# All scores of a pair in one four-bank tile, with wide exponentials and another order of the attention loop

## The chip, the cores and the metric

The kernel runs on one core of a Trainium2 chip. The core has a matrix engine (TensorE, called PE in the profile, with its weight loads as PEld), a vector engine (VectorE, DVE), a scalar engine (ScalarE, ACT), GpSimd (POOL) and a sync engine (SP) that issues DMAs. Each engine works through its own list of instructions in order; semaphores make one engine wait for another. Matmul results land in PSUM[...]. Everything else lives in SBUF. The metric is the device time in microseconds (us).

## The reference

Two parts follow each other. The first is attention in chunks: for each of 4 batches and 8 heads (768 positions, 64 dimensions), each chunk of 32 queries sees 8 memory rows, 16 positions before it, its own 32 and 8 after it.

```python
q_c   = q[:, :, c_start:c_end]
k_full = concat([mem_k, k[:, :, max(0, c_start-16):min(S, c_end+8)]])   # v_full likewise
a   = softmax(q_c @ k_full.T / sqrt(64))
out[:, :, c_start:c_end] = a @ v_full
```

The second is a gated MLP on the 128 tokens of each batch that score highest. With x the attention output as (4, 768, 512), per batch:

```python
scores  = x @ w_gate                     # (768,)
top_idx = argpartition(-scores, 128)[:128]
xe = x[top_idx]
ye = relu(xe @ w1) @ w2                  # 512 -> 1024 -> 512
out[top_idx] = xe + sigmoid(scores[top_idx])[:, None] * ye
```

## The kernel before

**Pairs.** The attention works on pairs of heads: 16 pairs n, four to a batch. Three groups of 16 transposes on TensorE bring q, k and v of a pair into the layout that the matmuls want. `tr_q(n)` writes p_q and ScalarE copies it to qT (L219). `tr_k(n)` writes p_t and VectorE copies it to kw (L232), into which GpSimd puts the memory keys (`mem_cols`, L224). `tr_v(n)` writes p_t and ScalarE copies it to vw (L242). `back_v(n)` transposes vw once more into p_v, and VectorE copies it to vc (L251). p_q and p_v share one buffer (pool pvv, tag "pv"); p_t is a single tile.

**Scores and values.** `scores(n, half)` multiplies keys and queries of four of the eight groups, 8 matmuls into a two-bank tile p_s, of which there are two, and then runs three exponentials on ScalarE (L271), one for each of the three positions c of a chunk in a group, since each c has its own mask as bias. Each covers 256 elements per partition and writes es. `values(n, half, fills)` multiplies es with vc into the one-bank tile p_w (12 matmuls, L292; its ones column gives the sums), and VectorE takes the reciprocal rd (L295) and writes the normalized rows to x (L296). `fills` asks for a matmul of zeros ahead of it (L116).

**The order of the loop.** The order on every engine is the order in which the program emits its work. Per pair n it is: scores(n+1, 0), tr_q(n+2), values(n, 0), tr_k(n+2), scores(n+1, 1), back_v(n+1), values(n, 1), tr_v(n+2). Loads of q, k and v in units of two pairs are issued by GpSimd four units ahead, with a cast from fp32 to fp16; the weights w1 and w2 come on the same queue.

**The MoE part between.** `hook(i)` stands at eight places of each pair, i = 8n to 8n+7, and emits the steps of `moe_steps(b)` that are due there. For a batch b they begin at the first pair of the next batch: six dot products with w_gate (junk, L335, VectorE), rows of the scores by transposes into brow (L346, copied by ScalarE, L352), the gate (an exponential on ScalarE, then four small VectorE steps, L361 to L365), six comparisons (gr, L373), 37 counting matmuls (L380, L383), mask and incl (L389, L391), slot and sel (L398, L405), then the indices (aux, L438; idx, L441) and an indirect DMA that gathers the 128 rows (xe, L412). Later come `m_rows` (transposes of xe, L419, copied to xeT by ScalarE), `m_ffn1` in two halves (L453; hT by ScalarE, L455) and `m_ffn2` (L462; y by ScalarE, L465), and a DMA that adds y to the output (L466). All these use a single one-bank tile p_m (`m_bank`, pool pmm); for the last batch, LAST, they use p_s tiles. `m_x16` (L340, ScalarE) makes an fp16 copy of x of the last batch, half of it at pair 14.

**The tail.** After pair 15 GpSimd issues the store of the last batch's x. VectorE does the dot products of LAST in two halves: the first two pairs' columns inside pair 15 (scrA), the rest after the loop (scrB), then their sum (L581). `m_rows` and the FFN of batch 2 stand there in TensorE's list ahead of counts, gather by matmul and FFN of LAST.

Of the kernel before, what the change touches and what calls it, by code (L numbers as in the profile page):

```python
# [26 lines left out]
def kernel(  # L27
# [13 lines left out]
    nc = tc.nc  # L41
# [9 lines left out]
    NB = 6  # L51
    HD = S * D
    NPR = B * NP
    SLOTS = 4
# [3 lines left out]
    att = ctx.enter_context(tc.tile_pool(name="att", bufs=4))  # L58
    xpool = ctx.enter_context(tc.tile_pool(name="xp", bufs=2))
    mod = ctx.enter_context(tc.tile_pool(name="mod", bufs=2))  # L60

    pss = ctx.enter_context(tc.tile_pool(name="pss", bufs=2, space=bass.MemoryType.PSUM))
    pxx = ctx.enter_context(tc.tile_pool(name="pxx", bufs=1, space=bass.MemoryType.PSUM))
    pvv = ctx.enter_context(tc.tile_pool(name="pvv", bufs=1, space=bass.MemoryType.PSUM))
    ptt = ctx.enter_context(tc.tile_pool(name="ptt", bufs=1, space=bass.MemoryType.PSUM))
# [83 lines left out]
    vcs, kws, vws = [], [], []  # L149
# [63 lines left out]
    def tr_q(n):  # L213
        if n >= NPR:
            return
        p_q = pvv.tile([128, 8, 128], F16, tag="pv", name="p_q")[:, :, 0:96]
        transposes(q16s, n, p_q)
        qT = att.tile([128, 96, 8], F16, tag="qT", name="qT")
        nc.scalar.copy(out=qT, in_=p_q.rearrange("p j t -> p t j"))  # L219
        qTs[n] = qT  # L220
# [32 lines left out]
    GROUPS = ((0, 1, 2, 6), (3, 4, 5, 7))  # L253
    ess = {}

    def scores(n, half, fills=0):
        if n >= NPR:
            return
        kw, qT = kws[n % SLOTS], qTs[n]
        qf = qT.rearrange("p t j -> p (t j)")  # L260
        p_s = pss.tile([128, 2, 512], FP, tag="ps", name="p_s")
        fill_into(p_s[:, 0, :], fills)
        for gi, g in enumerate(GROUPS[half]):
            for h in range(2):
                o = 64 * h
                nc.tensor.matmul(out=p_s[:, h, 96 * gi:96 * gi + 96], lhsT=kw[o:o + 64, g, :],  # L266
                                 rhs=qf[o:o + 64, 96 * g:96 * g + 96], start=True, stop=True)
        es = att.tile([128, 2, 4, 96], F16, tag="es", name="es")
        pv = p_s[:, :, 0:384].rearrange("p s (g t) -> p s g t", t=96)
        for c in range(3):  # L270
            nc.scalar.activation(out=es[:, :, :, 32 * c:32 * c + 32], in_=pv[:, :, :, 32 * c:32 * c + 32],  # L271
                                 func=AF.Exp, bias=maskb[:, c:c + 1], scale=0.125)
        ess[n, half] = es

    xs = {}

    def values(n, half, fills=0):
        b, pr = divmod(n, NP)
        if pr == 0 and half == 0:
            xs[b] = xpool.tile([128, NB, Dm], FP, tag="x", name=f"x{b}")  # L280
        es, vc = ess.pop((n, half)), vcs[n % SLOTS]
        if n == NPR - 1:
            p_w = pss.tile([128, 2, 512], FP, tag="ps", name="p_w")[:, 0, :]
        else:
            p_w = pxx.tile([128, 512], FP, tag="px", name="p_w")
        fill_into(p_w, fills)
        p_x = p_w[:, 0:390].rearrange("p (i h c) -> p i h c", i=3, h=2)
        for r0, r1, gis in ((0, 96, (0, 1, 2)), (96, 128, (3, 3, 3))):
            for i, gi in enumerate(gis):
                q0, q1 = (0, 96) if gi < 3 else (32 * i, 32 * i + 32)  # L290
                for h in range(2):
                    nc.tensor.matmul(out=p_x[r0:r1, i, h, :], lhsT=es[:, h, gi, q0:q1],  # L292
                                     rhs=vc[:, GROUPS[half][gi], h, 0:65], start=True, stop=True)
# [10 lines left out]
    mods = [MS() for _ in range(B)]  # L304
    outf = out.rearrange("b s d -> (b s) d")
    LAST = B - 1

    def m_bank(b, shape, dt=FP):

        if b == LAST:  # L310
            t = pss.tile([128, 2, 512], FP, tag="ps", name="p_l")
            return t
        return pmm.tile([128, 1, 512], FP, tag="pm", name="p_m")

    def m_store(b):
# [13 lines left out]
    def m_dot(b, bls, pr0=0, pr1=NP, dst=None):  # L329
        m, x = mods[b], xs[b]  # L330
        dst = m.scr if dst is None else dst
        for bl in bls:
            c0, c1 = 2 * D * pr0, 2 * D * pr1
            junk = mod.tile([128, Dm], FP, tag="junk", name="junk")
            nc.vector.scalar_tensor_tensor(out=junk[:, c0:c1], in0=x[:, bl, c0:c1], scalar=1.0, in1=wgb[:, c0:c1],  # L335
                                           op0=ALU.mult, op1=ALU.mult, accum_out=dst[:, bl:bl + 1])

    def m_x16(b, lo, hi, pr0=0, pr1=NP):
        c0, c1 = 2 * D * pr0, 2 * D * pr1
        nc.scalar.copy(out=mods[b].x16[:, lo:hi, c0:c1], in_=xs[b][:, lo:hi, c0:c1])  # L340
# [128 lines left out]
    def moe_steps(b):  # L469

        st = {}

        def at(i, f, *a):
            st.setdefault(i, []).append(lambda: f(b, *a))

        at(0, m_alloc)
        p = dict(dots=(0, 3, 6, 7, 8, 11), row0=13, row1=16, gate=17, cmps=(18, 19, 22, 23, 24, 27),
                 counts=(30, 30, 30, 31, 31, 31), mask=31, slot=34, sel=35, fetch=37, rows=54, ffn=(55, 57, 59))
        if b == LAST - 2:
            p.update(rows=46, ffn=(47, 48, 50))  # L480
        if b == LAST - 1:
            p = dict(dots=(0, 1, 3, 4, 6, 7), row0=9, row1=11, gate=12, cmps=(13, 14, 15, 17, 18, 19),
                     counts=(21, 21, 21, 22, 22, 22), mask=22, slot=24, sel=24, fetch=24)
        for i in range(NB):
            at(p["dots"][i], m_dot, (i,))
        at(p["row0"], m_row, 0, 4)
        at(p["row1"], m_row, 4, 6)
        at(p["row1"], m_gate_exp)
        at(p["gate"], m_gate)
        for i in range(NB):  # L490
            at(p["cmps"][i], m_cmp, (i,))
        for i in range(NB):
# [18 lines left out]
    def hook(i):  # L511
        for f in places.get(i, ()):
            f()
# [7 lines left out]
    fill(2)  # L521
    tr_v(0)
    fill(3)
    scores(0, 0)
    mem_rows(memv16, memvT)
    for n in range(3):
        mem_cols(vws[n], memvT, n)
    tr_q(1)
    fill(2)
    tr_k(1)  # L530
    scores(0, 1)
    fill(2)
    back_v(0)
    tr_v(1)
    fill(2)
    late_constants()
    scrA = mod.tile([128, NB], FP, tag="scrA", name="scrA")
    scrB = mod.tile([128, NB], FP, tag="scrB", name="scrB")
    for n in range(NPR):
        b, pr = divmod(n, NP)  # L540
        i = 8 * n
        nf = 0 if b == 0 or n in (10, 11, 13, 14) else 1
        if b >= 1 and pr == 0:
            m_store(b - 1)
        if n == 1:
            nc.sync.dma_start(out=wgb, in_=_dap(moe_w_gate, 0, [[0, 128], [1, Dm]]))
        if n == NPR - 2:
            m_alloc(LAST)
        scores(n + 1, 0)
        hook(i)  # L550
        if n == NPR - 1:
            m_dot(LAST, range(NB), 0, 2, scrA)
        if 3 <= n + 3 < NPR:
            mem_cols(vws[(n + 3) % SLOTS], memvT, n + 3)
        tr_q(n + 2)
        hook(i + 1)
        values(n, 0, nf)
        hook(i + 2)
        tr_k(n + 2)
        hook(i + 3)  # L560
        scores(n + 1, 1)
        if n == NPR - 2:
# [75 lines left out]
```

## Time and profile before

| | |
|---|---|
| device time, median of 3 runs | 139.72 us (138.43 to 141.23) |
| span of the profiled run | 137.4 us |
| busy, PE / DVE / ACT / POOL | 111.7 / 87.5 / 80.0 / 50.5 us |
| exponentials (L271) | 96, 38.8 us, 485 ns each |
| copies vw, qT on ScalarE | 962 and 813 ns each |
| one of pairs 1 to 3 | 4.67 us |
| pairs 4 to 7 | 22.1 us |
| last x of pair 15 | 111.9 us |

The busy times say how much each engine has to do; the waits say which engine stands still for which. An engine's idle time matters only if what it does next is awaited by others, so the table has to be read with the order of work above: a pair's time is the longest ring of waits through the engines, and that ring differs from the plain pairs of batch 0 to the pairs that carry MoE steps.

### The profile page before, as it was taken

What the parts mean: (1) busy time and instruction counts of PE and PEld (TensorE: products, weight loads), DVE (VectorE), ACT (ScalarE), POOL (GpSimd) and SP (SyncE); (2) the same over time, 40 slices, a digit from 0 to 9 for tenths busy, and PEclk for the clock granted to TensorE, in tenths of its full rate; (3) what the DMA queues carried; (4) which work ended last, traced back from release to release, by engine and by line L of the source; (5) the groups of instructions that cost most, each with busy time, mean ns of one, the idle gap of its engine ahead of it and who ended that gap; (6) DMA issues with size and microseconds to landing.
All of it is one profiled execution on the core that took longest, in us unless ns stands there. A gap on an engine that the chain in (4) does not pass through costs nothing.

```text
span 137.4 us, 4727 instructions
## 1 busy us (share of the span) xinstructions
PE 111.7 (81%) x2024; PEld 83.0 (60%) x2024; DVE 87.5 (64%) x280; ACT 80.0 (58%) x159; POOL 50.5 (37%) x84
## 2 busy tenths in 40 slices
PE   6997688977998978989997999897797897888500
PEld 2355376866777756867885858685656555458100
DVE  3444556574799399889738955997954896651000
ACT  4047958779779859565676947858748005153300
POOL 6996364352683634914200226121004140040130
PEclk9999999999999999995599999999999559999995
DMA  2999999999999999999991002973001439606050
GB/s 63 173 146 184 203 206 206 205 212 206 205 248 287 278 208 206 205 235 290 286 185 23 0 7 19 268 252 43 0 5 12 67 38 260 203 0 81 0 70 6
DMA packets 15397, 19.90 MB, mean 145 GB/s; under 512 B 848, under 2 KB 11536, under 8 KB 15376
## 3 DMA queue, kind: packets, MB, share of 16 engines
q0 software_dynamic: 12832, 14.62, 63.4%
q1 hardware_dynamic: 2544, 4.98, 11.0%
q8 instruction: 16, 0.26, 0.7%
q14 instruction: 5, 0.04, 0.1%
HBM read 24.25 MB, written 7.34 MB: 230 GB/s over the span
## 4 chain that ended last, share of the span: by engine, by line
PE 31%; DVE 15%; ACT 14%; issue 14%; DMA 14%; POOL 6%; POOLq 1%
ACT es L271 7%; DMA q<-in_q_dram 7%; PE p_w L292 7%; PE p_t L210 5%; PE p_v L250 4%; DMA xe<-out_dram,idx 3%; DMA out_dram<-y,idx 3%; DVE junk L335 3%; DVE x L296 3%; ACT qT L219 3%; PE p_w L116 3%; PE p_m L462 3%; PE p_m L453 2%; DVE gr L373 2%; PE p_m L383 2%
## 5 line engine op out<-in xcount | busy, mean ns | idle before, releaser
L271 ACT ACTIVATE es<-p_s,maskb 128x256 f16<-128x256 f32 x96 | 38.8, 485 | 3.2 <-PE p_s L266 3.1
L292 PEld LDWEIGHTS <-es 128*32 128x32 f16 (+1 forms) x384 | 22.1, 116 | 4.4 <-issue 0.7
L292 PE MATMUL p_w<-vc,es 128*32 128x65 f16 (+1 forms) x384 | 24.4, 208 | 0.0
L242 ACT COPY vw<-p_t 128x960 f16<-128x960 f16 x16 | 15.4, 962 | 14.5 <-PE p_t L210 14.5
L224 POOL COPY kw<-memkT 128x64 f16<-128x64 f16 x12 | 8.0, 666 | 36.4 <-DVE kw L232 36.4
L296 DVE TENSOR_TENSOR x<-p_w,rd 128x384 f32<-128x384 f32 x32 | 17.8, 558 | 1.1
L219 ACT COPY qT<-p_q 128x768 f16<-128x768 f16 x16 | 13.0, 813 | 7.4 <-PE p_q L210 7.4
L335 DVE SCALAR_TENSOR_TENSOR junk<-x,wgb 128x512 f32<-128x512 f32 (+1 forms) x30 | 16.2, 582 | 0.0
L466 POOL DMA_INDIRECT out_dram<-y,idx x4 | 6.5, 1635 | 24.7 <-ACT y L465 23.4
L295 DVE RECIPROCAL rd<-p_w 128x6 f32<-128x6 f32 x32 | 6.1, 191 | 12.5 <-PE p_w L292 12.1
L373 DVE TENSOR_SCALAR gr<-brow,scr 128x768 f16<-128x768 f32 x24 | 14.0, 623 | 0.1
L116 PE MATMUL p_f<-zeros 128*128 128x512 f16 x36 | 12.8, 496 | 1.3 <-DVE zeros L110 1.3
L250 PE MATMUL p_v<-ident,vw 128*128 128x128 f16 x128 | 10.2, 225 | 4.3 <-ACT qT L219 4.3
L251 DVE COPY vc<-p_v 128x1024 f16<-128x1024 f16 x16 | 11.0, 687 | 4.3 <-PE p_v L250 4.1
L232 DVE COPY kw<-p_t 128x1024 f16<-128x1024 f16 x16 | 10.9, 683 | 3.5 <-PE p_t L210 3.4
L266 PE MATMUL p_s<-qT,kw 64*128 64x96 f16 x256 | 11.3, 209 | 0.3 <-POOL kw L224 0.3
L250 PEld LDWEIGHTS <-vw 128*128 128x128 f16 x128 | 8.1, 100 | 5.6 <-issue 4.1
L116 PEld LDWEIGHTS <-zeros 128*128 128x128 f16 x60 | 5.9, 110 | 8.9 <-issue 4.6
L210 PE MATMUL p_q<-ident,q 96*64 96x96 f16 x256 | 8.8, 213 | 2.6 <-DMA q<-in_q_dram 2.5
L116 PE MATMUL p_w<-zeros 128*128 128x512 f16 x24 | 9.8, 410 | 1.0 <-DVE x L296 1.0
L210 PEld LDWEIGHTS <-q 96*64 96x64 f16 x256 | 6.7, 113 | 4.5 <-DMA q<-in_q_dram 2.7
L453 PEld LDWEIGHTS <-w_sb 128*128 128x128 f16 x128 | 7.6, 97 | 2.5 <-issue 1.6
(112 smaller groups left out, 165.0 us busy)
## 6 DMA issues: line engine op xcount, KB each, us to landing
out_dram<-x SPq DMA_DIRECT2D x3, 1152.0 KB, 11.5
k<-in_k_dram POOLq DMA_DIRECT2D x7, 384.0 KB, 13.2
q<-in_q_dram POOLq DMA_DIRECT2D x7, 384.0 KB, 13.7
v<-in_v_dram POOLq DMA_DIRECT2D x7, 384.0 KB, 14.6
w_sb<-in_moe_w_dram POOLq DMA_DIRECT2D x8, 256.0 KB, 13.4
out_dram<-x SPq DMA_DIRECT2D x3, 384.0 KB, 13.2
out_dram<-x POOLq DMA_DIRECT2D x1, 1152.0 KB, 6.8
k<-in_k_dram POOLq DMA_DIRECT2D x2, 192.0 KB, 4.8
```

The lines of the kernel that those rows point to most:

```text
L116: nc.tensor.matmul(out=ap, lhsT=zeros[:, 0:128], rhs=zeros, start=True, stop=True)
L210: nc.tensor.transpose(out=dst[64 * h:64 * h + 64, j, :], in_=src[n][:, h, 64 * j:64 * j + 64], identity=ident16[0:96, 0:96])
L219: nc.scalar.copy(out=qT, in_=p_q.rearrange("p j t -> p t j"))
L242: nc.scalar.copy(out=vw.rearrange("p g (j t) -> p g j t", t=16)[:, :, :, 0:15], in_=_sap(p_t, 0, [[12, NG], [100, 8], [1, 15]]))
L250: nc.tensor.transpose(out=p_v[:, g, :, :], in_=vws[n % SLOTS][:, g, :], identity=ident16)
L251: nc.vector.tensor_copy(out=vcs[n % SLOTS][:, :, :, 0:64], in_=p_v)
L266: nc.tensor.matmul(out=p_s[:, h, 96 * gi:96 * gi + 96], lhsT=kw[o:o + 64, g, :], rhs=qf[o:o + 64, 96 * g:96 * g + 96], start=True, stop=True)
L271: nc.scalar.activation(out=es[:, :, :, 32 * c:32 * c + 32], in_=pv[:, :, :, 32 * c:32 * c + 32], func=AF.Exp, bias=maskb[:, c:c + 1], scal ...
L292: nc.tensor.matmul(out=p_x[r0:r1, i, h, :], lhsT=es[:, h, gi, q0:q1], rhs=vc[:, GROUPS[half][gi], h, 0:65], start=True, stop=True)
L296: nc.vector.tensor_tensor(out=xs[b].rearrange("p g (n h d) -> p n g h d", n=NP, d=D)[:, pr, 3 * half:3 * half + 3], in0=p_x[:, :, :, 0:64] ...
L335: nc.vector.scalar_tensor_tensor(out=junk[:, c0:c1], in0=x[:, bl, c0:c1], scalar=1.0, in1=wgb[:, c0:c1], op0=ALU.mult, op1=ALU.mult, accum ...
L373: nc.vector.tensor_scalar(out=m.gr[:, bl, :], in0=m.brow, scalar1=m.scr[:, bl:bl + 1], scalar2=None, op0=ALU.is_lt)
```

## The change

Scores of a whole pair go to one four-bank tile p_s of which there is one instead of two tiles of two banks, so PSUM use is the same. `scores(n)` issues 16 matmuls at once, and three exponentials cover 512 elements per partition each instead of six of 256. In the loop, tr_q(n+2) comes first, then scores(n+1), and the two halves of values(n) stand around tr_k, back_v and ahead of tr_v. With p_s as a single tile, the last batch takes its banks one after the other from a four-bank tile (`last_bank`). The slot, sel and gather steps of batch 2 move from i = 24 to i = 30, so from the beginning of pair 15 to behind its second values. The dot products of LAST are done in one piece after the loop. The purpose is fewer ScalarE instructions and a shorter ring between ScalarE and TensorE.

```diff
-    pss = ctx.enter_context(tc.tile_pool(name="pss", bufs=2, space=bass.MemoryType.PSUM))
+    pss = ctx.enter_context(tc.tile_pool(name="pss", bufs=1, space=bass.MemoryType.PSUM))
...
-    def scores(n, half, fills=0):
+    def scores(n):
...
-        p_s = pss.tile([128, 2, 512], FP, tag="ps", name="p_s")
-        fill_into(p_s[:, 0, :], fills)
-        for gi, g in enumerate(GROUPS[half]):
-            for h in range(2):
-                o = 64 * h
-                nc.tensor.matmul(out=p_s[:, h, 96 * gi:96 * gi + 96], lhsT=kw[o:o + 64, g, :],
-                                 rhs=qf[o:o + 64, 96 * g:96 * g + 96], start=True, stop=True)
-        es = att.tile([128, 2, 4, 96], F16, tag="es", name="es")
-        pv = p_s[:, :, 0:384].rearrange("p s (g t) -> p s g t", t=96)
+        p_s = pss.tile([128, 2, 2, 512], FP, tag="ps", name="p_s")
+        for half in range(2):
+            for gi, g in enumerate(GROUPS[half]):
+                for h in range(2):
+                    o = 64 * h
+                    nc.tensor.matmul(out=p_s[:, half, h, 96 * gi:96 * gi + 96], lhsT=kw[o:o + 64, g, :],
+                                     rhs=qf[o:o + 64, 96 * g:96 * g + 96], start=True, stop=True)
+        es = att.tile([128, 2, 2, 4, 96], F16, tag="es", name="es")
+        pv = p_s[:, :, :, 0:384].rearrange("p a s (g t) -> p (a s) g t", t=96)
+        ev = es.rearrange("p a s g t -> p (a s) g t")
         for c in range(3):
-            nc.scalar.activation(out=es[:, :, :, 32 * c:32 * c + 32], in_=pv[:, :, :, 32 * c:32 * c + 32],
+            nc.scalar.activation(out=ev[:, :, :, 32 * c:32 * c + 32], in_=pv[:, :, :, 32 * c:32 * c + 32],
                                  func=AF.Exp, bias=maskb[:, c:c + 1], scale=0.125)
...
         if n == NPR - 1:
-            p_w = pss.tile([128, 2, 512], FP, tag="ps", name="p_w")[:, 0, :]
+            p_w = last_bank()
...
+    def last_bank():
+        if not last:
+            last.append(pss.tile([128, 4, 512], FP, tag="ps", name="p_l"))
+        last.append(None)
+        return last[0][:, len(last) % 4, :]
...
             p = dict(dots=(0, 1, 3, 4, 6, 7), row0=9, row1=11, gate=12, cmps=(13, 14, 15, 17, 18, 19),
-                     counts=(21, 21, 21, 22, 22, 22), mask=22, slot=24, sel=24, fetch=24)
+                     counts=(21, 21, 21, 22, 22, 22), mask=22, slot=30, sel=30, fetch=30)
...
-    scores(0, 0)
+    scores(0)
...
-    scores(0, 1)
...
-        scores(n + 1, 0)
+        tr_q(n + 2)
         hook(i)
-        if n == NPR - 1:
-            m_dot(LAST, range(NB), 0, 2, scrA)
-        if 3 <= n + 3 < NPR:
+        if n + 3 < NPR:
             mem_cols(vws[(n + 3) % SLOTS], memvT, n + 3)
-        tr_q(n + 2)
+        scores(n + 1)
+        if n == NPR - 2:
+            m_x16(LAST, 0, NB, 0, 2)
         hook(i + 1)
         values(n, 0, nf)
         hook(i + 2)
         tr_k(n + 2)
         hook(i + 3)
-        scores(n + 1, 1)
-        if n == NPR - 2:
-            m_x16(LAST, 0, NB, 0, 2)
         hook(i + 4)
         back_v(n + 1)
...
-    m_dot(b, range(NB), 2, 4, scrB)
-    nc.vector.tensor_tensor(out=mods[b].scr, in0=scrA, in1=scrB, op=ALU.add)
+    m_dot(b, range(NB))
```

More of the change, by code (lines that the diff above doesn't have):

```diff
@@ L260, in scores @@
         qf = qT.rearrange("p t j -> p (t j)")
-        p_s = pss.tile([128, 2, 512], FP, tag="ps", name="p_s")
-        fill_into(p_s[:, 0, :], fills)
-        for gi, g in enumerate(GROUPS[half]):
-            for h in range(2):
-                o = 64 * h
-                nc.tensor.matmul(out=p_s[:, h, 96 * gi:96 * gi + 96], lhsT=kw[o:o + 64, g, :],
-                                 rhs=qf[o:o + 64, 96 * g:96 * g + 96], start=True, stop=True)
-        es = att.tile([128, 2, 4, 96], F16, tag="es", name="es")
-        pv = p_s[:, :, 0:384].rearrange("p s (g t) -> p s g t", t=96)
+        p_s = pss.tile([128, 2, 2, 512], FP, tag="ps", name="p_s")
[8 more added lines that the diff above has]
+        ev = es.rearrange("p a s g t -> p (a s) g t")
         for c in range(3):
-            nc.scalar.activation(out=es[:, :, :, 32 * c:32 * c + 32], in_=pv[:, :, :, 32 * c:32 * c + 32],
+            nc.scalar.activation(out=ev[:, :, :, 32 * c:32 * c + 32], in_=pv[:, :, :, 32 * c:32 * c + 32],
                                  func=AF.Exp, bias=maskb[:, c:c + 1], scale=0.125)
-        ess[n, half] = es
+        ess[n] = es
     xs = {}
@@ L280, in values @@
             xs[b] = xpool.tile([128, NB, Dm], FP, tag="x", name=f"x{b}")
-        es, vc = ess.pop((n, half)), vcs[n % SLOTS]
+        es, vc = ess[n][:, half, :, :, :], vcs[n % SLOTS]
         if n == NPR - 1:
-            p_w = pss.tile([128, 2, 512], FP, tag="ps", name="p_w")[:, 0, :]
+            p_w = last_bank()
         else:
@@ L306 @@
     LAST = B - 1
+    last = []
+    def last_bank():
[3 more added lines that the diff above has]
+        return last[0][:, len(last) % 4, :]
     def m_bank(b, shape, dt=FP):
         if b == LAST:
-            t = pss.tile([128, 2, 512], FP, tag="ps", name="p_l")
-            return t
+            return last_bank().unsqueeze(1)
         return pmm.tile([128, 1, 512], FP, tag="pm", name="p_m")
@@ L536 @@
     late_constants()
-    scrA = mod.tile([128, NB], FP, tag="scrA", name="scrA")
-    scrB = mod.tile([128, NB], FP, tag="scrB", name="scrB")
     for n in range(NPR):
```

## The prediction

> **What bounds the kernel now.** I read the busy times and the slices first, then the waits and the chain of the plain attention stretch, then stretch after stretch, then the timeline where the chain leaves the loop.
>
> ```profile
> PE 111.7 (81%) x2024; PEld 83.0 (60%) x2024; DVE 87.5 (64%) x280; ACT 80.0 (58%) x159; POOL 50.5 (37%) x84
> ...
> PEclk9999999999999999995599999999999559999995
> DMA  2999999999999999999991002973001439606050
> ```
>
> No engine is full. The DMA engines are, from the second slice to about 74 us (slices of 3.43 us). The matmul clock is halved twice, near 61-68 and 106-113 us.
>
> Pairs 1 to 3 (21.25 to 35.2 us) repeat every 4.67 us. Their waits, and one turn of the chain:
>
> ```profile
> ACT vw L242 <- PE p_t L210: 2.2, 3, 0.8
> PE p_v L250 <- ACT qT L219: 2.1, 3, 0.7
> ...
> 21.29 0.29 ACT vw L242
> 21.58 0.56 issue
> 22.15 1.21 ACT es L271 x3
> 23.35 0.70 ACT qT L219
> 24.05 0.04 issue
> 24.09 0.61 PE p_v L250 x8
> ```
>
> It is a ring: copy vw, three exponentials, copy qT on ScalarE; then back_v (waiting 0.70 for qT, because p_q and p_v share one buffer), values and tr_v on TensorE; then the next vw. TensorE is busy 3.96 of 4.65 us, so 0.7 us a pair is what a better order can win here. Later pairs differ (columns: length, then busy PE, PEld, DVE, ACT, POOL):
>
> ```profile
> 25.90:30.55 4.65, 3.95 (x101) 3.34 (x101) 2.77 (x7) 3.86 (x8) 2.67 (x6) 1.00 1.21 209
> 39.90:45.00 5.10, 4.59 (x107) 3.88 (x105) 5.03 (x15) 4.44 (x9) 2.73 (x5) 1.00 1.10 283
> 51.40:57.30 5.90, 5.40 (x137) 4.42 (x135) 5.63 (x13) 4.05 (x9) 3.60 (x7) 1.00 1.24 205
> 77.40:85.40 8.00, 7.78 (x163) 5.98 (x159) 4.77 (x11) 5.19 (x11) 2.92 (x3) 1.00 0.04 6
> ```
>
> From pair 4 on VectorE carries the MoE work (5.0 of 5.1, 5.6 of 5.9 us), and pair 11 is TensorE's (7.8 of 8.0). ScalarE, which the change relieves, bounds neither. Two ScalarE stretches matter, around the FFNs of batches 0 and 1:
>
> ```profile
> 77.73 1.20 ACT L271 ACTIVATE es<-p_s,maskb 128x256 f16<-128x256 f32 x3
> 78.79 0.82 ACT L219 COPY qT<-p_q 128x768 f16<-128x768 f16 x1
> 79.47 0.64 ACT L455 ACTIVATE hT<-p_m 128x512 f16<-128x512 f32 x1
> ...
> 102.87 0.69 ACT L465 ACTIVATE y<-p_m,gate 128x512 f32<-128x512 f32 x1 [1.98 <-PE p_m L462]
> 103.46 1.20 ACT L271 ACTIVATE es<-p_s,maskb 128x256 f16<-128x256 f32 x3
> 104.52 1.49 ACT L340 CAST x<-x 128x1536 f16<-128x1536 f32 x1
> ```
>
> Today hT and y slip in between the two halves of the exponentials.
>
> [...] the trace has 485, and starts 0.36 apart. [...] the trace shows two halvings, no rule for them.
>
> **The change, part by part.** I carry one number, after minus before, at landmarks.
>
> *Exponentials.* Six of 256 elements become three of 512. [...] A pair: 6 x 0.36 = 2.16 becomes 1.72, so 0.44 us of ScalarE a pair, 7 us in all. The last result of the set is 1.85 us after the first start, not 1.2.
>
> *Pairs 0 to 3.* Pair 0: tr_q(2) waits for its load until 17.53 in both; now both score halves stand behind it instead of before it: +0.3. Then a pair costs TensorE tr_q 0.46, scores 0.56, values 2 x 0.67, tr_k 0.46, back_v 0.45, fill 0.22, tr_v 0.46 = 3.95. Does it wait? From the end of tr_v: vw is done at 1.07, qT at 1.8, and back_v's turn comes at 0.46 + 0.56 + 0.67 + 0.46 = 2.15: the 0.7 wait is gone. VectorE's vc ends just as tr_q wants the shared buffer: 0.05. The single p_s adds a wait, of scores(n+1) for the last exponential of pair n, with values, tr_k and back_v queued behind it; but that exponential precedes vw, which is read 1.07 after tr_v's end at the latest, and ended before it began: nothing. So 4.0 to 4.15 instead of 4.67: three pairs give 1.7. **At pair 4: -1.4.**
>
> *Pairs 4 to 9.* VectorE's list is unchanged: per pair rd/x 2 x 0.78, kw 0.63, vc 0.63 = 2.8, plus six junk x 0.62, gate 0.85, six gr x 0.6, mask and incl 0.35 over four pairs: 19.7 of 22.1 us. I lay the new order out with these durations, from tr_q to tr_q. Pair 4: the first junk ends at 1.2; values(4,0) ends at 0.46 + 0.56 + 0.22 + 0.67 = 1.9, so VectorE idles to 2.0, then rd/x 2.8, kw 3.4, junk 4.05, vc 4.7, for which the next tr_q waits: 4.75. Pair 5: rd/x, two junk, then junk, rd/x, kw, junk, vc without a gap to 10.0: 5.3. Pair 6: VectorE waits at 10.8 for the gate's exponential, behind qT and brow on ScalarE, to 12.1; then gate, rd/x, gr, kw, gr, vc to 16.1: 6.1. Pair 7 by the same way 5.9. Sum 22.05, against 57.3 - 35.2 = 22.1. A later start of values (both scores before it) eats what the shorter ring would give. **At pair 8: -1.4.** Full clock there could make it -3.
>
> *The first gather.* m_rows of batch 0 ran at 75.07. The gather it needs, seen alone:
>
> ```profile
> L412 POOL DMA_INDIRECT xe<-out_dram,idx x1: 1056/1056/1056, 62.9 to 62.9; - x1
> ...
> DMA to landing us min/median/max: 11.6/11.6/11.6
> ```
>
> It landed at 62.9 + 11.6 = 74.5, behind the last q, k, v loads on full DMA engines. Their bytes don't change, so it lands then again, and TensorE waits. **At rows(0): -0.6**, whatever was won before.
>
> *Pair 11.* hT's second half is now behind all of es(12). From rows at 74.5: ffn1 75.6-76.6, hT 77.3, qT 78.0, es 77.9-79.75, hT 80.2, ffn2 80.2-82.1 where it was 80.16-82.05; back_v, values and counts end at about 85.1 (85.1 before). The queue of wide exponentials takes the 0.6. **0.0.**
>
> *Pair 12.* VectorE runs without a gap from mask (85.23) to idx (91.16); the gather follows at 91.58. Now values(12,0) comes after both score halves, 0.35 of idling in that run. **Gather of batch 1: +0.4**, and its data 4.8 us later. *Pair 13.* The second m_row waits for brow, behind all of es(14) instead of a half; with qT first that is 0.4: **rows(1): +0.8.**
>
> *Pair 14.* After rows(1) (r): ffn1 to r+3.9 as before, scores(15) to r+4.45, es(15) to r+6.2 (next start), the 1.46 us x16 to r+7.65, only then y to r+8.35, which frees the one p_m buffer. The counts, and behind them values(14,1), start at r+8.45; before it was 103.61 - 96.40 = 7.2. **x(14,1): +2.0.**
>
> *Pair 15 and tail.* Before, from x(14,1) at 106.07: slot, sel and idx, six half junk (2.1), then x(15) until +5.9; gather issued at +3.24, rows(2) at +7.5. Now x(15) ends at +2.4, then slot, sel, idx: gather at about +4.3, landing between its 1.04 us on POOL and the at most 4.1 that the trace leaves (109.31 to 113.39); I take 3.2: rows(2) at +7.5. The six full junk (3.7) end at +7.9, just behind rows(2), so m_row follows without harm. From rows(2) on it is rows, ffn1, ffn2, counts in TensorE's order, as before. **End: +2.0.** Removed adds and the 0.17 sum of scrA and scrB lie beside TensorE's work and count nothing.
>
> 139.7 + 2.0 = 141.7 us, 1.4% slower.
>
> **Rivals.** (A) Faster: the page's chain passes through the store of x(15) and the final scatter; if that store really bound the end, x(15) earlier by 3.5 would count: 141.7 - 3.5 = 138.2. For it: the chain names it. Against: the scatter's wait is on y (7.71 us idle), not on the store. A bolder form, every pair at TensorE's floor as in pairs 1 to 3, gives 16 x 0.7 = 11, so 128.7; the nines of VectorE and the gather at 74.5 speak against. (B) Slower: TensorE idles some 2 us before rows(0), and longer before rows(1) and (2); if this costs one more half-speed window of 6.8 us in dense work, or the gather of batch 2 takes the 4.8 of batch 1's, add 1.5 to 3: 144. For it: two such windows in the trace; against: they came without long gaps. (C) The delays in pairs 11 to 14 are half of my 2.6: 140.4.
>
> **How the numbers follow.** Forecast and C 0.53, B 0.33, A 0.14 (of it 0.03 the bold form). Faster by over 2% means below 136.9: the bold form and the lower part of A, 0.11. Slower means above 142.5: most of B and a fifth of the forecast, 0.41. The rest 0.48. The range reaches below A's 138.2 to 137.5 and past B's 144 to 145, since a late gather and a slow window can add up.
>
> **What would show it.** es at about 700 ns; the wait of p_v for qT gone and pairs 1 to 3 near 4.0; pair 8 starting 1.4 earlier; rows(0) waiting for its DMA near 74.5; y of batch 1 after x16; x(15) soon after x(14), gather after it. I am wrong if pairs 4 to 7 shorten, if the loads end well before 74, or if the last FFN doesn't hang on the gather of batch 2.

## The result, and the profile after

The changed kernel takes 150.82 us (median of 4 executions, 147.74 to 154.51), the kernel before beside it 139.56 (138.43 to 141.23): 1.066 times as long, 95% interval 1.050 to 1.083. The forecast was 141.7, with a range of 137.5 to 145: slower was the right direction, but it had +2.0 us where +11.3 came. Medians below are over all executions of a kernel; ratios leave out those in which the chip ran the kernel slower than its own best by more than 1.5%.

The page of the changed kernel, the lines that answer to those shown of before, and the new exponentials (busy us, mean ns of one, idle before):

```profile
span 147.4 us, 4662 instructions
...
PE 113.6 (77%) x2024; PEld 84.6 (57%) x2024; DVE 86.1 (58%) x267; ACT 72.7 (49%) x111; POOL 50.1 (34%) x84
...
PEclk9999956999999999599999999999998555799995
DMA  2999999999999999999800079220050690040041
...
L272 ACT ACTIVATE es<-p_s,maskb 128x512 f16<-128x512 f32 x48 | 29.6, 695 | 0.2 <-PE p_s L266 0.2
```

The exponentials are as forecast: 695 ns each (forecast about 700), 48 of them, a set of three in 1.86 us, that is with starts 0.58 apart, and ScalarE's busy time falls from 80.0 to 72.7 us. The forecast's length was the author's estimate. The trace of the kernel before leads to it too: its copies into brow on ScalarE (L352) take 384 ns for 256 elements and 598 for 512, 0.84 an element, and 485 + 256 x 0.84 = 700. The exponentials, at 485 and 695, give 0.82.

TensorE does the same 2,024 matmuls in 113.6 instead of 111.7 us, but over 10 us more of span: it waits more. The row PEclk has fives, that is half of the full clock, early (slice 5 of 3.69 us, counted from 0), at 59 us and in three slices from 114 to 125 us. The DMA engines are full, or nearly so, for 20 slices (20 x 3.69 = 74 us; before 21 x 3.44 = 72).

The prediction carried one number, after minus before, at landmarks. Here it is with what was measured. The last column is an experiment told below, in which three parts of the change are taken back and the loop stays as changed. Each column is read from one profiled execution. "Rows" are the first transposes of the gathered rows, "last FFN" is the second layer of batch 3.

| landmark | before, us | forecast | changed kernel | changed loop alone |
|---|---|---|---|---|
| pair 4, tr_q(6) | 35.5 | -1.4 | +0.9 | -1.4 |
| pair 8, tr_q(10) | 57.3 | -1.4 | +0.9 | -1.2 |
| rows of batch 0 | 75.07 | -0.6 | 0.0 | -0.4 |
| rows of batch 1 | 96.40 | +0.8 | +1.5 | +2.9 |
| rows of batch 2 | 113.61 | +2.0 | +3.4 | +2.5 |
| counts of batch 3 | 120.22 | +2.0 | +7.5 | +3.1 |
| last FFN | 127.09 | +2.0 | +9.8 | +3.1 |

Up to the rows of batch 2 the changed kernel stays within 2.3 us of the ledger. (The +2.9 in the last column holds half-speed windows of its own, at 74.8 to 78.2 and 91.8 to 98.6 us.) Of the 9.8 us, 6.4 arise after the rows of batch 2, where the prediction had put nothing. The timeline of TensorE from pair 15 on in the changed kernel (start, us, engine, line, operation, count; in brackets the idle time before and what ended it):

```profile
109.77 0.38 PE L116 MATMUL p_l<-zeros 128*128 128x512 f16 x1 [0.88 <-DVE x L297]
...
119.14 0.69 PE L354 MATMUL p_l<-ident,scr 128*128 128x128 f32 x2 [0.68 <-ACT brow L360]
119.62 1.91 PE L461 MATMUL p_m<-xeT,w_sb 128*128 128x128 f16 x16
...
124.83 3.00 PE L470 MATMUL p_m<-w_sb,hT 128*128 128x512 f16 x8 [0.68 <-ACT hT L463]
```

and its m_row and FFN of batch 2 in the kernel before:

```profile
114.34 0.84 PE L346 MATMUL p_l<-ident,scr 128*128 128x128 f32 x6 [0.34 <-DVE scr L581]
115.02 1.06 PE L453 MATMUL p_m<-xeT,w_sb 128*128 128x128 f16 x16
...
118.50 1.89 PE L462 MATMUL p_m<-w_sb,hT 128*128 128x512 f16 x8 [0.69 <-ACT hT L455]
```

Two things happen. The second values of pair 15 wait 0.88 us for VectorE to read the first ones, and the second part of m_row waits 0.68 us for ScalarE to read the first part's result (brow), although in both cases the two lie in different banks (slices of 512 numbers of p_l); before, m_row is one group of 6. And ffn1 of batch 2 takes 1.91 us instead of the 1.06 of the kernel before, ffn2 3.00 instead of 1.89: the granted clock is 0.50 to 0.51 from 113.4 to 127.1 us and 0.99 in the 3.4 us behind. Then the FFN of the last batch, first in the changed kernel, then in the kernel before:

```profile
132.72 0.29 PE L446 MATMUL p_l<-aux,sel 128*128 128x3 f16 x6 [0.72 <-ACT xeT L440]
133.39 1.05 PE L461 MATMUL p_l<-xeT,w_sb 128*128 128x128 f16 x16 [0.37 <-DVE gate L451]
135.18 1.05 PE L461 MATMUL p_l<-xeT,w_sb 128*128 128x128 f16 x16 [0.73 <-ACT hT L463]
136.92 1.89 PE L470 MATMUL p_l<-w_sb,hT 128*128 128x512 f16 x8 [0.69 <-ACT hT L463]
```

```profile
124.39 0.29 PE L438 MATMUL p_l<-aux,sel 128*128 128x3 f16 x6
125.28 1.95 PE L453 MATMUL p_l<-xeT,w_sb 128*128 128x128 f16 x32 [0.60 <-ACT xeT L432]
127.09 1.90 PE L462 MATMUL p_l<-w_sb,hT 128*128 128x512 f16 x8
```

Before, the index matmuls (aux) run while ScalarE still copies xeT, both halves of ffn1 run as one group of 32 matmuls, and ffn2 starts right behind on the first half of hT. Now each of the four steps waits 0.37 to 0.73 us for ScalarE or VectorE to finish reading the step before. No data asks for most of this: aux doesn't read xeT, and ffn1's second half doesn't read hT (only ffn1's first half waited before, 0.60 us, for the xeT that it reads). The four p_l slices are one tile, and the waits are those that come if a step waits for the readers of the tile, not of the slice. From counts to the last scatter the kernel before took 9.79 us, the changed one 12.16.

### The profile page after: what moved, and what is told of

It is laid out like the page before. It is cut to its first block, busy times and chain, and to the rows that moved or that the text cites. A ratio compares the mean times of both kernels' runs of the same rounds, so it can differ in the third digit from the quotient of the medians.

```text
span 147.4 us, 4662 instructions
## 1 busy us (share of the span) xinstructions
PE 113.6 (77%) x2024; PEld 84.6 (57%) x2024; DVE 86.1 (58%) x267; ACT 72.7 (49%) x111; POOL 50.1 (34%) x84
## 4 chain that ended last, share of the span: by engine, by line
PE 32%; DMA 20%; issue 16%; DVE 12%; ACT 9%; POOL 5%; POOLq 1%; DVEq 0%
DMA xe<-out_dram,idx 10%; PE p_w L293 8%; DMA q<-in_q_dram 7%; PE p_t L210 4%; ACT es L272 4%; PE p_q L210 3%; DMA out_dram<-y,idx 3%; PE p_s L266 3%; PE p_w L116 3%; PE p_v L250 2%; DVE x L297 2%; DVE kw L232 2%; PE p_m L461 2%; DVE gr L381 2%; PE p_m L391 2%
## 5 line engine op out<-in xcount | busy, mean ns | idle before, releaser
L272 ACT ACTIVATE es<-p_s,maskb 128x512 f16<-128x512 f32 x48 | 29.6, 695 | 0.2 <-PE p_s L266 0.2
L293 PE MATMUL p_w<-vc,es 128*96 128x65 f16 (+1 forms) x360 | 22.8, 207 | 0.6 <-issue 0.6
L297 DVE TENSOR_TENSOR x<-p_w,rd 128x384 f32<-128x384 f32 x30 | 16.7, 558 | 1.0
L343 DVE SCALAR_TENSOR_TENSOR junk<-x,wgb 128x512 f32<-128x512 f32 x24 | 15.8, 695 | 0.0
L116 PE MATMUL p_f<-zeros 128*128 128x512 f16 x36 | 11.9, 466 | 1.3 <-DVE zeros L110 1.3
L210 PEld LDWEIGHTS <-q 96*64 96x64 f16 x256 | 7.6, 115 | 8.6 <-DMA q<-in_q_dram 5.3
L461 PEld LDWEIGHTS <-w_sb 128*128 128x128 f16 x128 | 9.2, 110 | 3.7 <-issue 3.4
L116 PE MATMUL p_w<-zeros 128*128 128x512 f16 x22 | 9.0, 407 | 0.9 <-DVE x L297 0.9
L461 PE MATMUL p_m<-xeT,w_sb 128*128 128x128 f16 x96 | 8.0, 250 | 1.9 <-ACT hT L463 1.4
L429 ACT COPY xeT<-p_e 128x512 f16<-128x512 f16 x3 | 1.8, 585 | 15.3 <-PE p_e L427 15.3
## 6 DMA issues: line engine op xcount, KB each, us to landing
q<-in_q_dram POOLq DMA_DIRECT2D x7, 384.0 KB, 13.7
```

Source lines behind the costliest of these rows:

```text
L210: nc.tensor.transpose(out=dst[64 * h:64 * h + 64, j, :], in_=src[n][:, h, 64 * j:64 * j + 64], identity=ident16[0:96, 0:96])
L272: nc.scalar.activation(out=ev[:, :, :, 32 * c:32 * c + 32], in_=pv[:, :, :, 32 * c:32 * c + 32], func=AF.Exp, bias=maskb[:, c:c + 1], scal ...
L297: nc.vector.tensor_tensor(out=xs[b].rearrange("p g (n h d) -> p n g h d", n=NP, d=D)[:, pr, 3 * half:3 * half + 3], in0=p_x[:, :, :, 0:64] ...
L461: nc.tensor.matmul(out=p_h[:, 0, 128 * fi:128 * fi + 128], lhsT=w1_sb[:, dch, f0:f0 + 128], rhs=m.xeT[:, dch, :], start=(dch == 0), stop=( ...
```

## The experiments

Each of the first four starts from the changed kernel; on their chip the kernel before took 142.41 us (139.0 to 145.75). Only two of its seven executions there, 139.0 and 139.1, stand in the ratios, so these are rough and have no interval.

**Separate banks for the last batch.** Only the slices go: the LAST steps use two tiles in turn.

```diff
-        if not last:
-            last.append(pss.tile([128, 4, 512], FP, tag="ps", name="p_l"))
         last.append(None)
-        return last[0][:, len(last) % 4, :]
+        if len(last) % 2:
+            return pss.tile([128, 4, 512], FP, tag="ps", name="p_l")[:, 0, :]
+        return pvv.tile([128, 512], FP, tag="pv", name="p_l")
```

> The changed kernel, with only the last batch's PSUM banks altered: instead of slices of one four-bank tile, two tiles in turn (one bank of p_s, and the p_v bank that is free by then). Theory (false waits): a slice of the one tile waits for readers of its other slices, so TensorE stood 0.88 us before the second values of pair 15, 0.68 us inside m_row and 2.4 us from the counts to the last scatter; they go, about 4 us faster than the change, 1.03 times the time before. Rival (clock): the tail's loss is the two half-speed windows at 113 to 127 us alone, and the time stays within 1 us of the change.

144.55 us (144.11 to 145.41), 1.04 times the kernel before. Aux follows the gather matmuls without a wait, ffn1 is one group of 32 again (1.95 us), the wait of 0.88 in pair 15 is gone, and the time from the slot matmul to the last FFN is shorter by 2.4 us (5.34 against 7.72; the kernel before has 5.34). Of the parts that were tried alone, the slices are the largest loss.

**More fills in the tail.** Matmuls of zeros where TensorE idles from pair 14 on.

```diff
+        if n == NPR - 2:
+            fill(4)
         hook(i + 5)
...
-    fill(8)
+    fill(13)
```

(And fill(4) and fill(5) around values(15, 1).)

> The changed kernel with matmuls of zeros put where TensorE stood idle near the end: 4 ahead of the counts of pair 14, 4 and 5 around the second values of pair 15, 13 instead of 8 ahead of the last m_rows. Theory (clock): the idle spots let the clock drop at 113 us for two windows, which cost about 4 us between 117 and 128 us; kept busy, the clock stays full and the end comes 3 to 4 us earlier, the spans agreeing better from run to run. Rival (false waits): same time or up to 1 us slower, since the fills only lengthen the queue.

149.9 us (147.17 to 152.33), 1.07 times the kernel before: no gain. The 13 fills ran out before the gather of batch 2 landed, TensorE idled 1.17 us, and a half-speed window came at 120 us all the same.

**Slot of batch 2 early and dot products split, as before; slices kept.**

```diff
-  counts=(21, 21, 21, 22, 22, 22), mask=22, slot=30, sel=30, fetch=30)
+  counts=(21, 21, 21, 22, 22, 22), mask=22, slot=24, sel=24, fetch=24)
...
+        if n == NPR - 1:
+            m_dot(LAST, range(NB), 0, 2, scrA)
...
-    m_dot(b, range(NB))
+    m_dot(b, range(NB), 2, 4, scrB)
+    nc.vector.tensor_tensor(out=mods[b].scr, in0=scrA, in1=scrB, op=ALU.add)
```

> The changed kernel with pair 15 as before the change: slot, sel and the gather of batch 2 back at step 24, the dot products of the last batch again in two halves. Theory: the gather of batch 2 goes out near 111 instead of 113.5, so m_rows of batch 2 runs 1 to 2 us earlier and the end with it. Rival: x of pair 15 comes 3.5 us later again and the end does not move or comes later.

147.45 us (146.84 to 149.6), 1.06 times the kernel before. The rows of batch 2 don't come earlier: in the profiled execution the gather went out at 112.57, 0.9 earlier than in the changed kernel, but the rows began at 118.91, 1.9 later (a half-speed window from 111.9 to 118.7 us adds to it). They stand behind TensorE's own work this time: VectorE does the slot steps and the dot products ahead of reading the first half of values(15), and the second half, a slice of the same tile, waits for that reading:

```profile
114.34 0.58 PE L116 MATMUL p_l<-zeros 128*128 128x512 f16 x1 [2.23 <-DVE x L297]
```

**Both of them: separate banks and early slot.** What is left of the change is the loop.

> Both undone, the banks and pair 15: what is left of the change is the wide exponentials, the four-bank score tile and the order of the loop. If the loop itself is worth what the prediction gave it (x of pair 14 later by 2.0 us, measured 2.5), the time is 1.01 to 1.025 times the time before. If the loop carries the loss, it stays near 1.06.

143.96 us (143.08 to 145.95). The median is 1.5 us above that of the kernel before; with the executions that the ratios take it is 143.7 against 139.0, 1.03 times. So the loop is not free. With and without slices, at the early slot, is 147.45 against 143.96: 3.5 us for the slices. The late slot costs 0.6 with separate banks (144.55 against 143.96), which the ranges don't separate from nothing.

The next four ran on another chip, where the kernel before took 140.59 us (139.1 to 142.76).

**The slices alone, put into the kernel before.** One two-bank tile is taken once for LAST, and last_bank() hands out its two slices in turn.

```diff
         if b == LAST:
-            t = pss.tile([128, 2, 512], FP, tag="ps", name="p_l")
-            return t
+            return last_bank().unsqueeze(1)
```

> The kernel before with one thing changed: the banks of the last batch are the two slices of one two-bank tile instead of two tiles in turn. Nothing else differs, no order, no size. Theory (each use of a slice waits for the readers of the other slice): ffn1 of the last batch splits around a wait of about 0.7 for hT, ffn2 waits 0.7, the second m_row 0.7, the aux matmuls 0.7 for xeT; 2.5 to 4 us longer than the kernel before on the same chip, with almost all of it after rows(2). Rival (waits follow the bytes of each slice, and the losses of the changed tail are the clock's): same as before within 0.5 us at equal clock.

147.04 us (143.52 to 152.19), 1.034 times the kernel before (1.019 to 1.049). TensorE's tail in this kernel:

```profile
129.99 0.29 PE L445 MATMUL p_l<-aux,sel 128*128 128x3 f16 x6 [0.72 <-ACT xeT L439]
130.65 1.05 PE L460 MATMUL p_l<-xeT,w_sb 128*128 128x128 f16 x16 [0.37 <-DVE gate L450]
132.44 1.86 PE L460 MATMUL p_l<-xeT,w_sb 128*128 128x128 f16 x16 [0.73 <-ACT hT L462]
134.99 3.57 PE L469 MATMUL p_l<-w_sb,hT 128*128 128x512 f16 x8 [0.68 <-ACT hT L462]
```

The same four waits, to 0.01 us, in a kernel in which nothing else differs; the durations 1.86 and 3.57 are a half-speed window on top. The second values of pair 15 (1.74 us) and the second part of m_row (0.68) wait as well. This settles the slices.

**y of batch 1 ahead of x16.** From the version with both parts undone:

```diff
-        if n == NPR - 2:
-            m_x16(LAST, 0, NB, 0, 2)
         hook(i + 1)
         values(n, 0, nf)
         hook(i + 2)
+        if n == NPR - 2:
+            m_x16(LAST, 0, NB, 0, 2)
```

> The version with separate last banks and the early slot of batch 2 (whose loop is that of the changed kernel), with one line moved: the copy x16 of pair 14 is issued after the second FFN layer of batch 1 instead of before it. Theory (what remains of the loss is y of batch 1 queued behind the exponentials and the copy x16 on ScalarE): y comes about 1.4 us earlier after rows(1), the idle of 0.99 us ahead of the counts goes, and the kernel takes about 142.8 against 144.0 without the move, that is about as long as the kernel before on the same chip. Rival (the gather of batch 2 or x16 itself sets the end): y earlier, the end within 0.4 of 144.0.

142.76 us (141.73 to 143.78), 1.024 times the kernel before (1.012 to 1.036). The version without the move was not run on this chip; its two near relatives below took 144.09 and 144.3. ScalarE and TensorE around y, in the changed kernel and here:

```profile
104.06 1.48 ACT L348 CAST x<-x 128x1536 f16<-128x1536 f32 x1
...
105.42 0.70 ACT L473 ACTIVATE y<-p_m,gate 128x512 f32<-128x512 f32 x1
106.18 0.17 PE L388 MATMUL p_m<-zero,ltri 128*128 128x6 f16 x1 [0.99 <-ACT y L473]
```

```profile
106.16 0.69 ACT L473 ACTIVATE y<-p_m,gate 128x512 f32<-128x512 f32 x1 [0.60 <-PE p_m L470]
...
106.75 1.46 ACT L348 CAST x<-x 128x1536 f16<-128x1536 f32 x1
106.90 0.17 PE L388 MATMUL p_m<-zero,ltri 128*128 128x6 f16 x1 [0.33 <-ACT y L473]
```

The idle of 0.99 ahead of the counts falls to 0.33. The forecast's order for pair 14 (x16, then y, then the counts) is what the first of the two shows. Without x16 between them the counts begin 7.59 us behind the rows of batch 1 and not 8.25, that is 0.65 earlier, not 1.4 as expected: y now waits for ffn2. The time is 1.2 to 1.5 us below that of the relatives; what is more than 0.65 of it isn't shown to come from this line.

This kernel is also the last column of the table: its early part had the full clock. TensorE's transposes of q at the starts of pairs 0, 1 and 4, in the changed kernel and here:

```profile
18.01 0.85 PE L210 MATMUL p_q<-ident,q 96*64 96x96 f16 x16 [1.98 <-DMA q<-in_q_dram]
...
24.33 0.70 PE L210 MATMUL p_q<-ident,q 96*64 96x96 f16 x16
...
36.42 0.51 PE L210 MATMUL p_q<-ident,q 96*64 96x96 f16 x16
```

```profile
17.70 0.53 PE L210 MATMUL p_q<-ident,q 96*64 96x96 f16 x16 [2.23 <-DMA q<-in_q_dram]
...
21.67 0.53 PE L210 MATMUL p_q<-ident,q 96*64 96x96 f16 x16
...
34.07 0.51 PE L210 MATMUL p_q<-ident,q 96*64 96x96 f16 x16
```

From pair 1 to pair 4 both take 12.1 to 12.4 us, that is 4.0 to 4.1 a pair as forecast. The changed kernel lost 2.35 us in pair 0, in which its clock was halved (17.8 to 24.7 us).

**Fills ahead of the loop's first tr_q.** 14 instead of 2, in the version with both parts undone.

> The same base, with 14 fill matmuls of zeros instead of 2 ahead of the loop's first tr_q, where TensorE idles some 2 us for the load of q. Theory (the idle brings the half-speed window near 17 us, and what is lost or won before rows(0) is given back there, because the gather of batch 0 lands behind the loads near 74.5): the early window goes, pair 4 starts near 34 to 35 instead of 36.4, rows(0) waits for its gather near 75, and the end stays within 0.7 of 144.0. Rival 1 (the early gain is carried to the end): about 142. Rival 2 (windows come whatever TensorE does): the window stays.

144.09 us (142.53 to 146.37). The half-speed window didn't go, it came earlier (13.4 to 16.8), and the fills overran the load, so that pair 4 began at 35.56. The rows of batch 0 waited for their gather until 74.96. The changed kernel and seven of the versions wait for that gather, and their rows(0) begin at 73.9 to 75.2, while their pair 4 begins anywhere from 33.8 to 37.1. In the two kernels and the first four versions the gather of batch 0 goes out at 61.9 to 65.8 us and lands at 73.8 to 75.2; it takes 11.9 us where it goes out first and 9.1 where it goes out last. Going out 3.9 us earlier landed it 1.1 earlier. It is a gate: the eight traces that wait for it stand still for it for 0.30 to 2.71 us.

**Narrow exponentials in the new order.** Two sets of three half-width ones from the same tile.

```diff
+        for a in (0, 2):
             for c in range(3):
-                nc.scalar.activation(out=ev[:, :, :, 32 * c:32 * c + 32], ...
+                nc.scalar.activation(out=ev[:, a:a + 2, :, 32 * c:32 * c + 32], ...
```

> The version with separate last banks and the early slot, its three wide exponentials a pair written again as two sets of three half-width ones (same order, same four-bank tile). ScalarE gets about 7 us more work. Theory (ScalarE is not the bound, the wide exponentials bring and cost nothing): within 0.7 of 144.0. Rival (the wide form matters): either 1 to 2 us slower because the ring qT, vw gets later, or faster because values(n,0) can start after the first half.

144.3 us (143.37 to 146.18), 1.030 times the kernel before (1.018 to 1.042), where the wide form on the other chip had 1.03: no difference that can be measured. The 7 us of ScalarE time that the wide form saves are not seen in the time, as forecast.

The last seven ask what the lead before the gate could be made of. The first four had a kernel before of 140.95 us (137.84 to 145.16) beside them, the other three 141.22 (138.54 to 146.06).

**Rows of batch 0 later.** From the version with y first:

```diff
+        if b == 0:
+            p.update(rows=56, ffn=(57, 59, 61))
```

> The version with separate last banks, the early slot and y ahead of x16, with the rows of batch 0 and its FFN moved a few hooks later (rows 54 to 56, FFN 55, 57, 59 to 57, 59, 61), so that the transposes of v and q for pairs 12 and 13 fill the idle time of 2.3 us before the gather has landed. Theory (the loop reaches rows(0) early and throws the lead away waiting, and the idle brings a half-speed window just in the FFN): the wait before rows(0) falls below 1.5, the FFN of batch 0 runs at full speed (ffn1 halves 1.05), and the end comes 0.7 to 1.5 earlier than without the move, 141.3 to 142 where that measured 142.8 and the kernel before 140.6. Rival (later work is VectorE's, and the end does not move): within 0.5 of the version without the move.

142.48 us (141.07 to 144.92), 1.025 times the kernel before (1.016 to 1.033). The wait before rows(0) is gone and the FFN runs at full speed (ffn1 1.05), so the mechanism is as expected; but half-speed windows come at 90 and 111 us, and the end isn't measurably earlier.

**Fills ahead of rows(0).** fill(8) there, in the version with y first.

> The same base (separate last banks, early slot, y ahead of x16), with 8 fill matmuls of zeros (about 1.7 us) ahead of rows(0) in place of the idle, and no work moved. Theory (idle time is what brings the half-speed window at rows(0)): ffn1 of batch 0 takes 1.05 a half, not 1.89, the mask of batch 1 comes about 1 us earlier, 141.8 or so. Rival (windows come regardless of idle time, as the fills in the tail suggested): the window stays, 142.8.

145.79 us (144.06 to 148.25), 1.042 times the kernel before (1.033 to 1.050). This one missed its aim:

```profile
76.37 3.60 PE L116 MATMUL p_f<-zeros 128*128 128x512 f16 x8 [2.02 <-DVE x L297]
```

The fills write the bank of the values, so they waited 2.02 us for VectorE to read x out of it and ended at 80 us. The idle stayed, and rows(0) began behind them at 79.76, with no wait for its gather and 5 us later than without them.

**tr_q ahead of the scores in the kernel before,** with narrow halves and all else as it was.

> The kernel before with one line moved: the transposes tr_q stand ahead of the first half of the scores. No other part of the change. Theory (the ring of pairs 0 to 3 gets its 0.7 a pair from qT's place in ScalarE's queue, and it is lost at rows(0)): back_v no longer waits for qT, pair 4 starts 1 to 1.5 earlier than 35.5, rows(0) waits for its gather until 74.7, and the time is within 0.7 of the kernel before. Rival 1 (the lead is kept): 1.4 faster. Rival 2 (the longer idle at rows(0) costs a half-speed window): 1 to 2 slower.

143.83 us (141.01 to 145.76), 1.025 times the kernel before (1.013 to 1.037). Pair 4 begins at 33.83, and back_v no longer waits for qT, so the order of the two in ScalarE's queue is what shortens the ring; and the kernel gets slower. In the profiled execution the lead is not lost at the gate, as was expected: two half-speed stretches (51.4 to 54.8 and 61.6 to 68.5 us) use it up before, and rows(0) begins at 76.23 without a wait. Its mean clock is 0.872 over six executions, the kernel before has 0.913 over 25.

**The same with the rows later.**

> The kernel before with tr_q ahead of the scores and with the rows of batch 0 and its FFN moved later by the same hooks (56 and 57, 59, 61). Theory (the lead of the shorter ring counts once other work stands before rows(0)): 0.5 to 1.4 us faster than the kernel before on the same chip. Rival (VectorE and the gate set pairs 8 to 12): same.

150.5 us (146.51 to 151.31), mean clock 0.845. A clear miss. In its profile a half-speed window runs from 52 to 72 us, rows(0) comes at 82.0 and its FFN is at half speed too.

**Fills that wait for nobody.** In the version with y first, 9 fills ahead of rows(0), written into the MoE bank, which has no reader then.

```diff
+        if b == 0:
+            fill_into(pmm.tile([128, 512], FP, tag="pm", name="p_f"), 9)
```

> The version with separate last banks, the early slot and y ahead of x16, with 9 fill matmuls of zeros ahead of rows(0), written into the MoE bank, which nobody reads then, so that they start at once (the earlier fills stood in the bank of the values and waited 2.0 us for VectorE). No work is moved. Theory (a half-speed window of the matmul clock follows a stretch in which TensorE idled): the 2.3 us of idle go, no half window begins at 75, the FFN of batch 0 runs its halves of ffn1 in 1.05 instead of 1.89, and batch 1's counts come at 83 to 83.5 instead of 84.7. Rival (windows come regardless of idle, or dense fills bring them): ffn1 at 1.9 and counts at 84.7 or later.

141.69 us (141.13 to 143.81), 1.011 times the kernel before (1.002 to 1.020). TensorE at rows(0) with y first but no fills, and here:

```profile
74.70 0.54 PE L427 MATMUL p_e<-ident,xe 128*128 128x128 f16 x4 [2.30 <-DMA xe<-out_dram,idx]
...
75.95 1.89 PE L461 MATMUL p_m<-xeT,w_sb 128*128 128x128 f16 x16
```

```profile
73.23 2.12 PE L116 MATMUL p_f<-zeros 128*128 128x512 f16 x9
...
76.46 1.05 PE L463 MATMUL p_m<-xeT,w_sb 128*128 128x128 f16 x16 [0.21 <-ACT xeT L431]
```

In the first TensorE idles 2.30 us, and the next window is at half speed: ffn1 takes 1.89. In the second the same stretch is filled, and ffn1 takes 1.05. The counts of batch 1 come 0.5 earlier, less than the 1.2 or more expected, since rows(0) now starts 0.7 later, behind the fills. Each of the two is one profiled execution. This is the best version with the changed loop, and it is still not faster than the kernel before.

**Fills in pairs 12 and 14,** 3 each ahead of aux of batches 1 and 2 and of the slot matmul of batch 2, in the banks that these write anyway; once in the version with rows later, once in the kernel before.

> The version with rows of batch 0 moved later (142.5 against 141.0 of the kernel before, beside it), with 3 fill matmuls of zeros in front of the aux matmuls of batches 1 and 2, and 3 in front of the slot matmul of batch 2, in the very banks these write, where TensorE idles 0.6 to 0.9 us at a time for VectorE's incl and sel. Theory (idle brings half windows): the windows at 90 and 111 go, the FFNs of batch 1 and 2 keep full speed, mean clock above 0.92, and the time falls by 1.5 to 3 to 139.5 to 141. Rival: the windows stay or move elsewhere and the time stays at 142.5 or above.

147.93 us (144.53 to 150.47), 1.041 times the kernel before (1.024 to 1.058): slower, not faster. Half-speed windows came at 101 and 122 us instead of 90 and 111.

> The kernel before with the same 9 fill matmuls (3 ahead of the aux matmuls of batch 1, 3 of batch 2, 3 ahead of the slot matmul of batch 2) and nothing else. Theory (idle brings half windows): fewer windows after 85, mean clock higher than that of the kernel before on the same chip, and 0.5 to 2 us faster. Rival: no difference within 0.5 us, or slower by the fills' own time, up to 1 us.

142.29 us (139.24 to 147.36), 1.007 times the kernel before (1.000 to 1.014): nothing gained. No version tried beats the kernel before.

## Why the prediction was wrong, step by step

- **Exponentials, ring, pairs 0 to 3.** Right: 695 ns, 4.0 to 4.1 us a pair, back_v's wait for qT gone, pair 4 at -1.4 where the clock was full. In the profiled execution of the changed kernel a half-speed window in pair 0 turned it into +0.9.
- **Pairs 4 to 9, first gather, -0.6 at rows(0).** Right: -1.2 at pair 8 with the full clock, and the gate held, with the idle time that the forecast expected ("TensorE waits"). The row of nines only shows that the DMA engines are full, to about 72 us before and 74 after; that the gather stands behind their loads fits its landings (73.8 to 75.2 for issues from 61.9 to 65.8), but wasn't shown by itself. The waiting can be paid for again, as rival B had it: with y first, TensorE idled 2.3 us there and the clock was halved in the FFN behind it. In the profiled execution of the changed kernel, which had lost its lead, the wait was 0.49 and ffn1 took the full-speed 1.05.
- **Pair 14, +2.0.** Right: the counts come 8.25 behind the rows of batch 1 (forecast 8.45, before 7.2), with x16 ahead of y, and x(14,1) is 2.5 later. One moved line takes 0.65 of it back.
- **Pair 15.** The gather of batch 2 was put at +4.3 from x(14,1). It was issued at 113.47, 4.9 behind x(14,1), 0.6 later than forecast, and the second values(15), ahead of the slot matmul on TensorE, had waited 0.88 for the first one's reader (the shared tile again; with separate banks the gather goes out 6.35 us behind the counts of batch 2 and not 7.29). It landed after 3.5 (taken: 3.2).
- **End: the step that failed** is "From rows(2) on it is rows, ffn1, ffn2, counts in TensorE's order, as before." The order is as before; the waits are not. The forecast gave last_bank no term: the waits of the tail were put at nothing more than before, without a reason. In the trace, 0.68 (brow) and about 2.4 between counts and the last scatter come from slices of one tile, and the two experiments on slices give 3.5 us one way and 3.4% (1.9 to 4.9) the other.
- **The rest of the tail, some 2.8 us,** is clock: ffn1 and ffn2 of batch 2 at half speed (1.91 + 1.86 + 3.00 instead of 1.06 + 1.05 + 1.89). Rival B named one more such window of 6.8 us as the way to 144, and priced it at 1.5 to 3, which is what the one in pair 0 cost (2.35). The tail had two of that length in a row. Up to its last matmul the profiled execution had 23.9 us at half speed, that of before 13.7.

How much is clock and how much order can be split with the 25 executions of the kernel before beside the first twelve experiments. Their spans lie on a line against their mean clock: span = 198.7 - 64.8 x clock, with 0.8 us of scatter about it (spans of 137.4 to 137.9 us at 0.960, of 142.9 to 143.9 at 0.862); 29 more executions on another chip, beside the last three, lie 0.05 us below it in the mean, with the same scatter. Against this line, that is at an equal clock, the changed kernel is 6.1 us longer, the version without slices 3.0, without the late slot 4.7, with neither 0.9, with y first 0.8, and tr_q moved in the kernel before -0.3. So at an equal clock the changed loop costs about 1 us, the tail's parts some 5, the slices 3 to 4 of them. The remaining 3.6 us of the changed kernel are the lower clock (0.858 over its four executions, against 0.913). Two of the four, at 0.80 and 0.82, lie below the clocks that the line was fitted to. The line shows that time and clock go together, not that the clock is apart from the change: every version with the changed loop has a mean clock from 0.86 to 0.91. Which part of the change lowers it stays open: filling one idle stretch removed one window; filling others moved them.

## What to carry to other kernels

Give steps that should overlap separate tiles: in this program slices of one tile, though in banks of their own, waited for one another's readers, 0.37 to 0.73 us a step in the tail. Before crediting a shorter loop, look for the next gate (here a gather that landed at 73.8 to 75.2 us) and ask what the engine does while it waits; a lead that turns into idle time can be lost twice, as with y first, where TensorE idled 2.30 us and a half of ffn1 behind it took 1.89 us instead of 1.05. Put fills into a bank without readers, or they wait themselves, as here for 2.02 us.

## What was not expected of the hardware

The forecast said that the trace shows "no rule" for half-speed windows. Seventeen traces together show a strong tendency. The granted clock changes at the borders of slots of 3.41 us: in the kernel before it is 1.00 in the slot up to 61.61 us, 0.51 and 0.50 in the next two, 0.99 in the one from 68.44. I cut each trace, from 14 to 125 us, into these slots (the clock is 0.50 to 0.53 or 0.97 to 1.00 in every one), and took the matmuls' busy share of each full-speed slot, and whether the next was at half speed:

| busy share of the slot | slots | followed by half speed |
|---|---|---|
| under 0.60 | 27 | 20 |
| 0.60 to 0.75 | 81 | 28 |
| 0.75 to 0.90 | 146 | 9 |
| 0.90 and more | 177 | 1 |

A slot need not be idle to be followed by half speed: 48 of the 108 with a busy share under 0.75 were, and 10 of the 323 above. It is a correlation over the traces, with one stretch tried in both ways (rows(0) with y first, idle and filled: ffn1 1.89 and 1.05 us). What such a stretch costs is about what its matmuls take longer: 2.35 us for 6.8 us at half speed in pair 0, 2.8 us in the FFN of batch 2 (7.5 us of a stretch of 13.7).
